# One attention and mixing kernel on one core: 24 float32 tiles of 32, smaller groups for scaling v, two weight tiles moved, all first shifts planned, filler products on TensorE

## The chip, the cores and the metric

One core of one Trainium2 chip. The metric is the device time of one execution, in microseconds (us); a profiled execution also gives a trace with every instruction of TensorE (PE), VectorE (DVE, Vector), ScalarE (ACT, Act), GpSimdE (POOL, Pool) and of the DMA queue of SyncE (SP).

## The reference

Three layers in a row. An attention over 2 batches of 8 heads, 768 rows of 64: query and key bits are the signs of six projections, and a score counts only where all six bits agree; then a softmax and the weighted sum of v. A channel layer with a time shift: `xk` and `xr` are mixtures of x and the row before it, `k = relu(xk @ w_k)`, `v = k*k @ w_v`, and the result is `sigmoid(xr @ w_r) * v`. A mixing layer: `u = x + (x^T U V)^T`, and the output is `u + relu(u @ w_ch1) @ w_ch2`. The weights reach the kernel as float64.

```python
mask = q_bucket[:, :, :, None] == k_bucket[:, :, None, :]
scores = np.where(mask, scale * np.matmul(q, k.transpose(0, 1, 3, 2)), -1000000000.0)
attn = np.exp(scores - np.max(scores, axis=-1, keepdims=True))
attn = attn / (np.sum(attn, axis=-1, keepdims=True) + 1e-09)
x = np.matmul(attn, v)                                   # then by batch, row, head*64
v = np.maximum(xk @ w_k, 0.0) ** 2 @ w_v
x = v / (1.0 + np.exp(-(xr @ w_r)))
u = x + (x.transpose(0, 2, 1) @ U @ V).transpose(0, 2, 1)
out = u + np.maximum(u @ w_ch1, 0.0) @ w_ch2
```

## The kernel before, in words

**Attention.** 16 heads of 6 query tiles, 96 tiles n = 6i + t. For each head q and k are loaded, split into a high and a low part (`prep_H`, `prep_L`), transposed on TensorE (`prep_T`), copied (`prep_E`), and the bits are made from a product (`prep_z`, `prep_bits`) and put beside the operands by DMA. For each tile: scores in four products of 384 columns (`scores`, lines 511 and 512), the row maximum on Vector (`row_max`, line 516) with two small steps, and the exponential on Act (`exps`, line 530). From there a tile goes one of two ways. A D tile is split into two fp16 parts (`part1` on Pool or Act, `part2` on Pool), transposed by a DMA (`transp`) and weighted with v in 18 fp16 products (line 577). A W tile (t = 1 and 4, `PE_TILES`) is transposed by TensorE in float32 (`flip`, line 556), copied out of PSUM by Act or Vector (`flip_out`) and weighted in 6 float32 products, 12 instructions (line 571). The sums of a head lie in one PSUM bank, `o`; at the head's end Vector reads it twice (`total`, line 584, and `normal`, line 596, with the reciprocal, line 588, between).

**v.** A power of two scales v for four heads together (`VG = 4`): Vector takes the largest value of each head's v (`v_max`, line 464), TensorE transposes the four maxima (`v_flip`, line 470), Vector makes the factor (`v_power`), TensorE spreads it (`v_spread`), Vector copies it (`v_scale`, line 487), and Act scales each head's v (line 496) before any tile of these heads can be weighted.

**Weights.** Each float64 weight tile is turned into two float32r parts in a chain: load, `conv_scale` on Act, `conv_bits` on Vector, `conv_sum` on Pool, and a split on Act and Vector or Pool. The first `JOBS = 8` tiles are made inside the attention; the others in ticks of the later loops, one stage of each per tick.

**The order.** The instructions of the attention are put in order by a planner (`Plan.order`, lines 75 to 125). It lists operations with costs for each engine, what they follow, which buffers (`SLOTS`) they take and free, and a due time (`DUE`, added to a step number); at each moment it starts what is ready and due first. Each engine runs its instructions in that order, so a wait holds everything behind it on that engine.

**The first shifts.** The channel layer of batch 0 needs 16 shifted inputs (`Mix.todo`: r and k, two halves of the rows, four chunks), each of which is scaled, summed, copied by Act (`shift_high`) and completed by Pool or Vector (`shift_low`). Twelve are in the plan, with the products for r (`r_step`); the last four, the second half for k, come after it, between the first half unit `k_half(mix, 0)` and the others. A unit m has two halves u = 2m and 2m + 1; the order of the halves, `u1`, is 0, 2, 1, 3, 4, ... The second products of a half (line 797 to 799, 9 of 512 columns) follow the first ones (12 of 384 columns) of the next half. The mixing layer at the end has 16 steps m for each group g of four row tiles, with the remaining weight tiles in ticks of g = 0.

## Time and profile before

| | us |
|---|---|
| median of 3 runs (739.63 to 741.1) | 739.86 |
| the profiled execution | 737.28 |
| its span, first to last instruction | 735.1 |
| busy in the span: PE, DVE, ACT, POOL | 701.2, 441.8, 384.8, 350.7 |
| mean granted clock of TensorE | 0.984 |

The attention ends at about 284 us, where the first unit of the channel layer starts. TensorE is busy for 95% of the span; busy times of products overlap, since they are pipelined, so the distance between starts tells more of their cost than their lengths. The trace names a line of the kernel and the tiles that an instruction writes and reads: `ps` and `pt` are PSUM tiles, `pT` a transposed tile, `xh` a split shifted input, `hl` a split first product, `nv` v in float32.

### The profile page before, as it was taken

What the parts mean: (1) busy time and instruction counts of PE and PEld (TensorE: products, weight loads), DVE (VectorE), ACT (ScalarE), POOL (GpSimd) and SP (SyncE); (2) the same over time, 40 slices, a digit from 0 to 9 for tenths busy, and PEclk for the clock granted to TensorE, in tenths of its full rate; (3) what the DMA queues carried; (4) which work ended last, traced back from release to release, by engine and by line L of the source; (5) the groups of instructions that cost most, each with busy time, mean ns of one, the idle gap of its engine ahead of it and who ended that gap; (6) DMA issues with size and microseconds to landing.
All of it is one profiled execution on the core that took longest, in us unless ns stands there. A gap on an engine that the chain in (4) does not pass through costs nothing.

```text
span 735.1 us, 12021 instructions
## 1 busy us (share of the span) xinstructions
PE 701.2 (95%) x4556; PEld 604.6 (82%) x4556; DVE 441.8 (60%) x791; ACT 384.8 (52%) x651; POOL 350.7 (48%) x308
## 2 busy tenths in 40 slices
PE   6879999998999998899999999999999999999997
PEld 6779988998899987788788888777888888888886
DVE  5868888777866575899779987845622111221112
ACT  3767878877878684676468656534421101210110
POOL 3879989876987774566347544623300000000000
PEclk9879999999999999899999999999999999999999
DMA  6688998898798792322012332322201000010001
GB/s 175 159 170 157 202 201 175 189 182 173 158 174 144 167 193 39 115 97 70 28 49 95 121 109 86 108 85 83 98 1 57 1 1 0 1 57 1 1 0 58
DMA packets 140714, 73.20 MB, mean 100 GB/s; under 512 B 116833, under 2 KB 134065, under 8 KB 140657
## 3 DMA queue, kind: packets, MB, share of 16 engines
q1 hardware_dynamic: 140512, 72.24, 42.1%
q8 instruction: 36, 0.59, 0.3%
q14 instruction: 22, 0.17, 0.1%
q10 hardware_dynamic: 144, 0.20, 0.1%
HBM read 37.10 MB, written 3.15 MB: 55 GB/s over the span
## 4 chain that ended last, share of the span: by engine, by line
PE 68%; POOL 10%; issue 6%; DVE 6%; DMA 5%; ACT 4%; SPq 0%; POOLq 0%; ACTq 0%; DVEq 0%
PE ps L797 9%; PE ps L799 9%; PE pt L797 9%; PE pt L799 9%; PE ps L798 9%; PE pt L798 9%; POOL p L179 4%; DMA pT<-p 3%; PE pt L571 3%; POOL p L381 2%; PE pt L577 2%; PE ps L511 2%; PE ps L512 2%; PE pt L405 1%; DVE w L179 1%
## 5 line engine op out<-in xcount | busy, mean ns | idle before, releaser
L872 DVE SCALAR_TENSOR_TENSOR hl<-pt,hl 128x512 fp32r<-128x512 f32 x48 | 33.2, 691 | 170.9 <-ACT hl L871 170.9
L871 ACT ACTIVATE hl<-pt 128x512 fp32r<-128x512 f32 x48 | 28.7, 598 | 186.1 <-PE pt L799 186.1
L799 PE MATMUL ps<-w,hl 128*128 128x512 f32 x288 | 114.3, 397 | 3.5 <-DVE hl L786 3.3
L797 PE MATMUL ps<-w,hl 128*128 128x512 f32 x288 | 115.6, 401 | 0.1
L798 PE MATMUL ps<-w,hl 128*128 128x512 f32 x288 | 113.7, 395 | 0.0
L179 POOL TENSOR_TENSOR cx<-cx,raw 128x512 int32<-128x512 int32 (+2 forms) x55 | 80.3, 1460 | 65.2 <-DVE cx L232 60.8
L179 POOL TENSOR_TENSOR p<-p,p 128x768 f16<-128x768 f32 x64 | 108.0, 1691 | 6.3 <-ACT p L379 4.5
L516 DVE TENSOR_REDUCE nm<-ps 128x1 f32<-128x768 f32 x96 | 90.5, 952 | 21.2 <-PE ps L512 19.2
L530 ACT ACTIVATE p<-ps,nm 128x768 f32<-128x768 f32 x96 | 92.8, 989 | 12.5 <-DVE nm L524 12.0
L511 PE MATMUL ps<-xk,xq 76*128 76x384 f32 x192 | 72.8, 379 | 3.4 <-ACT p L530 2.4
L797 PE MATMUL pt<-ut,w 128*128 128x512 f32 x192 | 75.6, 394 | 0.0
L799 PE MATMUL pt<-ut,w 128*128 128x512 f32 x192 | 75.0, 390 | 0.0
L798 PE MATMUL pt<-ut,w 128*128 128x512 f32 x192 | 75.0, 390 | 0.0
L799 PEld LDWEIGHTS ps<-w,hl 128*128 128x128 f32 x288 | 54.4, 189 | 19.4 <-DVE hl L786 7.4
L512 PE MATMUL ps<-yk,yq 128*128 128x384 f32 x192 | 67.2, 350 | 0.0
L797 PEld LDWEIGHTS ps<-w,hl 128*128 128x128 f32 x288 | 54.5, 189 | 14.2 <-issue 1.7
L179 DVE TENSOR_TENSOR w<-cx,w 128x512 fp32r<-128x512 f32 (+2 forms) x52 | 60.6, 1165 | 7.5 <-ACT w L272 7.1
L798 PEld LDWEIGHTS ps<-w,hl 128*128 128x128 f32 x288 | 54.6, 189 | 10.3
L577 PE MATMUL pt<-v,pT 128*128 128x65 f16 (+1 forms) x1152 | 47.3, 196 | 7.2 <-DMA pT<-p 5.2
L228 DVE SCALAR_TENSOR_TENSOR raw<-raw 128x512 uint32<-128x512 uint32 (+2 forms) x55 | 53.5, 973 | 0.0
L577 PEld LDWEIGHTS <-pT 128*128 128x128 f16 x1152 | 40.9, 99 | 13.9 <-issue 6.9
L381 POOL CAST p<-p 128x768 f16<-128x768 f32 x49 | 41.4, 846 | 22.1 <-ACT p L530 22.1
(178 smaller groups left out, 1478.1 us busy)
## 6 DMA issues: line engine op xcount, KB each, us to landing
raw<-in_moe_w_ch_dram SPq DMA_DIRECT2D x32, 512.0 KB
raw<-in_moe_w_k_dram SPq DMA_DIRECT2D x8, 512.0 KB
raw<-in_moe_w_v_dram SPq DMA_DIRECT2D x8, 512.0 KB
nk<-in_k_dram SPq DMA_DIRECT2D x16, 192.0 KB
nv<-in_v_dram SPq DMA_DIRECT2D x16, 192.0 KB
nq<-in_q_dram SPq DMA_DIRECT2D x15, 192.0 KB
xk<-yk SPq DMA_DIRECT2D x15, 192.0 KB
xq<-yq SPq DMA_DIRECT2D x15, 192.0 KB
```

The costliest lines, as they stand in the source:

```text
L179: eng.tensor_tensor(out=out, in0=a, in1=b, op=op)
L228: nc.vector.scalar_tensor_tensor(out=raw[:, :, 0], in0=raw[:, :, 1], scalar=0x80000000, in1=raw[:, :, 0], op0=ALU.bitwise_and, op1=ALU.bit ...
L381: (nc.vector if e == "dve" else nc.gpsimd).tensor_copy(dst, src)
L511: nc.tensor.matmul(s_ps[:, j, 0:G], d["xq"][:, qc], d["xk"][:, c], start=True, stop=False)
L512: nc.tensor.matmul(s_ps[:, j, 0:G], d["yq"][:, qc], d["yk"][:, c], start=False, stop=True)
L516: nc.vector.tensor_reduce(out=nm[:, 0:1], in_=tl[n]["s"][:, :, 0:G], axis=AX.XY, op=ALU.max, negate=True)
L530: nc.scalar.activation(p, tl[n].pop("s")[:, :, 0:G], AF.Exp, bias=nm[:, 2:3], scale=nm[:, 1:2])
L577: nc.tensor.matmul(o[:, 0:d], pT[:, part, kt, :], V[:, kt, a, 0:d], start=(kt == 0 and (part, a) == (0, 0)), stop=(kt == NT - 1 and part = ...
L797: nc.tensor.matmul(o, sh, mh, start=first, stop=False)
L798: nc.tensor.matmul(o, sh, ml, start=False, stop=False)
L799: nc.tensor.matmul(o, sl, mh, start=False, stop=last)
L872: nc.vector.scalar_tensor_tensor(out=hl[:, 1], in0=self.o, scalar=0.0, in1=f(hl)[:, 0], op0=ALU.max, op1=ALU.subtract)
```

## The change

- Tiles: `MODES` gives the way of each tile by batch and t. Batch 0 is D D W D D W, batch 1 is D D F D D W. An F tile is transposed by TensorE like a W tile; then Act takes its fp16 part out of PSUM (`flip_part1`), Vector subtracts it for the second part (`flip_part2`), and it is weighted by the 18 fp16 products of a D tile. So 24 of the 32 tiles that TensorE transposes stay float32.
- v is scaled in groups of 2, 2, 4, 4 and 4 heads (`GROUPS`).
- `JOBS` is 6: two weight tiles fewer in the attention. Two ticks (m = 4 and 6) are added in the mixing layer.
- All 16 first shifts are in the plan; the last four (`far`) wait for all scores and flips, because their buffers (`xh2`) take the place of the q and k preparation, whose tiles now have a pool of their own (`prep`) that is closed after the last score. The loop behind the plan is gone, and `u1` begins 0, 1, 2, ...
- Filler: before each operation of TensorE in the plan's order, a number of fp16 products of 128 x 128 ones with 120 columns is issued, 0.85 of the gap that the plan has there at 0.056 us each, and 34 ahead of the first. They write 120 spare columns of the bank of `o`, which is now one tile, `o_bank`, for all heads.
- The planner's costs of some operations and all due times are others.

```diff
@@ -20,18 +20,20 @@
 
-PE_TILES = (1, 4)
-DUE = {"ld": -28.3, "h": 7, "lo": 111.2, "tr": -11.5, "es": -25.5, "xs": 92.5, "z": -68.8, "bits": 0,
-       "mask": -276.3, "vm": -9.4, "v1": 6.8, "v2": -54.9, "sc": 55.7, "mx": 0.4, "sl": -2.6, "bi": -135,
-       "ex": 6.1, "fl": 48.2, "f1": 4.7, "p1": 52.8, "p2": 82.4, "T": -8, "av": 363.1, "nr": -62, "xp": 3.2,
-       "xe": -76.7, "j0": 20.9, "j1": 71.8, "j2": 329.8, "j3": 106.3, "j4": 470.2, "j5": 730.2, "j6": 845.8,
-       "j7": 172.1, "m0": -307, "m1": -117.4, "m2": 176.7, "r0": 344, "r1": 397.9, "r2": -42.6, "r3": -432.1,
-       "r4": -59.5, "r5": -145.5}
+MODES = ("DDWDDW", "DDFDDW")
+DUE = {"ld": -99.6, "h": -34.1, "lo": 130.6, "tr": 66.1, "es": -60.4, "xs": 46.6, "z": -218.4,
+       "bits": -138.8, "mask": -88.8, "vm": 17.4, "v1": 182.1, "v2": 335.9, "sc": 119.5, "mx": 10.9,
+       "sl": -3.2, "bi": -133.2, "ex": -22.6, "fl": 123.8, "f1": -95.5, "p1": 277.5, "p2": -1.3, "T": -77.7,
+       "av": 404.8, "nr": -45.7, "xp": 84.8, "xe": -119.1, "j0": 364.9, "j1": 212.6, "j2": 685.7,
+       "j3": 1005.2, "j4": 600, "j5": 738.7, "j6": 1882.5, "j7": -9.5, "m0": 30.4, "m1": -333.7, "m2": 373.4,
+       "r0": 351.9, "r1": 378, "r2": -841.9, "r3": -1555.3, "r4": -36.2, "fw": -86, "f2": -186.2,
+       "m3": 404.1, "r5": 0.4}
 JOB_GATE = (0, 0, 1, 1, 2, 3, 4, 5)
-JOBS = 8
-VG = 4
+JOBS = 6
+GROUPS = (2, 2, 4, 4, 4)
+FILL, FIRST_FILL = 0.85, 34
 SLOTS = {"s": 3, "t": 1, "o": 1, "n": 4, "hl_q": 1, "hl_k": 1, "y_q": 2, "y_k": 2, "x_q": 2, "x_k": 2, "zt": 2,
-         "p": 3, "p12": 4, "pT": 6, "xn": 2, "raw": 3, "cx": 4, "xh": 4, "sq": 3, "v": 2, "nm": 4, "nv": 6}
+         "p": 3, "p12": 4, "pT": 6, "xn": 2, "raw": 3, "cx": 4, "xh": 4, "xh2": 4, "sq": 3, "v": 2, "nm": 4, "nv": 6}
 
...
@@ -314,6 +318,8 @@
         nc.sync.dma_start(out=p_raw[r0:r0 + D, :], in_=proj)
+    steady = const.tile([128, 128], F16)
+    nc.gpsimd.memset(steady, 1.0)
     warm = const.tile([128, 1], F32)
...
@@ -321,6 +327,13 @@
     nc.gpsimd.tensor_copy(ident_r, ident)
+    o_bank = psum_t(512, "o")
+    spare = o_bank[:, NT * E1:NT * E1 + 120]
+
+    def idle_products(n):
+        for _ in range(n):
+            nc.tensor.matmul(spare, steady, steady[:, 0:120], start=True, stop=True)
+
     sgn = {"q": (-1.0, 1.0), "k": (1.0, -1.0)}
...
@@ -455,10 +468,12 @@
 
-    vg = [{} for _ in range(NH // VG)]
+    vg = [{} for _ in GROUPS]
+    vg_of = [(g, j) for g, n in enumerate(GROUPS) for j in range(n)]
+    VG = max(GROUPS)
 
     def v_max(i):
-        g, j = divmod(i, VG)
+        g, j = vg_of[i]
         if j == 0:
...
@@ -467,27 +482,28 @@
         vg[g]["t"] = psum_t()
-        nc.tensor.transpose(vg[g]["t"][0:VG, 0:128], vg[g].pop("max"), ident)
+        nc.tensor.transpose(vg[g]["t"][0:GROUPS[g], 0:128], vg[g].pop("max")[:, 0:GROUPS[g]], ident)
 
     def v_power(g):
-        m = ap.tile([VG, 1 + VG], F32, tag="vpow", name="vpow")
-        vg[g]["pow"] = m[:, 1:1 + VG]
+        n = GROUPS[g]
+        m = ap.tile([VG, 1 + VG], F32, tag="vpow", name="vpow")[0:n]
+        vg[g]["pow"] = m[:, 1:1 + n]
         m1 = m[:, 0:1]
-        nc.vector.tensor_reduce(out=m1, in_=vg[g].pop("t")[0:VG, 0:128], axis=AX.X, op=ALU.max)
+        nc.vector.tensor_reduce(out=m1, in_=vg[g].pop("t")[0:n, 0:128], axis=AX.X, op=ALU.max)
         nc.vector.tensor_scalar(m1, m1, 2.0 ** -100, None, ALU.max)
         nc.vector.tensor_scalar(words(m1), words(m1), 0x7F800000, 0x7F800000, ALU.bitwise_and, ALU.bitwise_xor)
-        nc.vector.tensor_scalar(vg[g]["pow"], ident[0:VG, 0:VG], m1, None, ALU.mult)
+        nc.vector.tensor_scalar(vg[g]["pow"], ident[0:n, 0:n], m1, None, ALU.mult)
 
     def v_spread(g):
         vg[g]["u"] = psum_t()
-        nc.tensor.matmul(vg[g]["u"][:, 0:VG], big, vg[g].pop("pow"), start=True, stop=True)
+        nc.tensor.matmul(vg[g]["u"][:, 0:GROUPS[g]], big[0:GROUPS[g]], vg[g].pop("pow"), start=True, stop=True)
 
     def v_scale(g):
-        sc = vg[g]["scale"] = ap.tile([128, VG], F32, tag="vsc", name="vsc", bufs=3)
-        nc.vector.tensor_copy(sc, vg[g].pop("u")[:, 0:VG])
+        sc = vg[g]["scale"] = ap.tile([128, VG], F32, tag="vsc", name="vsc", bufs=4)
+        nc.vector.tensor_copy(sc[:, 0:GROUPS[g]], vg[g].pop("u")[:, 0:GROUPS[g]])
 
     def v_scale_of(i):
-        g, j = divmod(i, VG)
+        g, j = vg_of[i]
         return vg[g]["scale"][:, j:j + 1]
...
@@ -510,6 +528,10 @@
             nc.tensor.matmul(s_ps[:, j, 0:G], d["yq"][:, qc], d["yk"][:, c], start=False, stop=True)
+        scored.append(n)
+        if len(scored) == NH * NT:
+            prep_s.close()
+            late["xh2"] = pool(mix_s, "xh2", bufs=4)
 
...
@@ -555,17 +577,33 @@
 
+    def mode(n):
+        return MODES[n // (NT * H)][n % NT]
+
     def flip_out(n, e):
         pT = tl[n]["pF"] = ap.tile([128, NT, 128], F32, tag="pT", name="pF", bufs=SLOTS["pT"])
         copy(e, pT.rearrange("p (j i) c -> p j (i c)", j=NG), tl[n].pop("f")[:, :, 0:G])
 
+    def flipped(n, part):
+        return tl[n]["pT"][:, part].rearrange("p (j i) c -> p j (i c)", j=NG), tl[n]["f"][:, :, 0:G]
+
+    def flip_part1(n):
+        pT_tile(n)
+        p1, src = flipped(n, 0)
+        nc.scalar.activation(p1, src, AF.Copy)
+
+    def flip_part2(n):
+        p1, src = flipped(n, 0)
+        minus("dve", flipped(n, 1)[0], src, p1)
+        tl[n].pop("f")
+
 
     def weighted(n):
         i, t = divmod(n, NT)
         if "o" not in hd[i]:
-            hd[i]["o"] = psum_t(NT * E1, "o").rearrange("p (t d) -> p t d", t=NT)
+            hd[i]["o"] = o_bank[:, 0:NT * E1].rearrange("p (t d) -> p t d", t=NT)
         o = hd[i]["o"][:, t]
-        if t in PE_TILES:
+        if mode(n) == "W":
             pT, v = tl[n].pop("pF"), NV[i % len(NV)]
...
@@ -945,18 +983,19 @@
         v_slots[i] = v_s, nv_s = Slot("v"), Slot("nv")
-        g, j = divmod(i, VG)
+        g, j = vg_of[i]
         ld = v_ld[i] = add({"sp": 0.74}, lambda e, i=i: load_head(i, "v"), ready_of[i - 4][1] if i >= 4 else [ld],
                            i * NT - 26 + 3 * j, take=[nv_s], issue=0.45)
         v_mx.append(add({"dve": 0.56}, lambda e, i=i: v_max(i), [ld], i * NT + 2 * j, "vm"))
-        if j == VG - 1:
-            at0 = g * VG * NT - 4
+        if j == GROUPS[g] - 1:
+            i0 = i - j
+            at0 = i0 * NT - 4
             t_s, u_s = Slot("t"), Slot("t")
-            fl = add({"pe": 0.2}, lambda e, g=g: v_flip(g), v_mx[-VG:], at0, take=[t_s], lag=0.25)
-            pw = add({"dve": 1.3}, lambda e, g=g: v_power(g), [fl], at0, free=[t_s])
+            fl = add({"pe": 0.2}, lambda e, g=g: v_flip(g), v_mx[i0:], at0, take=[t_s], lag=0.25)
+            pw = add({"dve": 1.5}, lambda e, g=g: v_power(g), [fl], at0, free=[t_s])
             sp = add({"pe": 0.2}, lambda e, g=g: v_spread(g), [pw], at0, take=[u_s], lag=0.25)
             v_sc = add({"dve": 0.15}, lambda e, g=g: v_scale(g), [sp], at0, free=[u_s])
-            for ii in range(g * VG, i + 1):
+            for ii in range(i0, i + 1):
                 v_s2, nv_s2 = v_slots[ii]
...
@@ -975,18 +1014,22 @@
             ex = add({"act": 1.02}, lambda e, n=n: exps(n), [bi], n, "ex", [p_s], [s_s, nm_s])
-            if t in PE_TILES:
+            kind = mode(n)
+            if kind in "FW":
                 f_s = Slot("s")
                 fl = add({"pe": 0.68}, lambda e, n=n: flip(n), [ex], n, "fl", [f_s], [p_s], lag=0.25)
                 last_s.append(fl)
-                got = add({"act": 0.83, "dve": 0.86}, lambda e, n=n: flip_out(n, e), [fl], n, "f1", [pT_s], [f_s])
+            if kind == "F":
+                p1 = add({"act": 0.83}, lambda e, n=n: flip_part1(n), [fl], n, "f1", [pT_s])
+                got = add({"dve": 0.97}, lambda e, n=n: flip_part2(n), [p1], n, "f2", free=[f_s])
+            elif kind == "W":
+                got = p1 = add({"act": 0.83, "dve": 0.95}, lambda e, n=n: flip_out(n, e), [fl], n, "fw", [pT_s], [f_s])
             else:
                 c_s = Slot("p12")
                 p1 = add({"act": 0.86, "pool": 0.85}, lambda e, n=n: part1(n, e), [ex], n, "p1", [c_s])
                 p2 = add({"pool": 1.7}, lambda e, n=n: part2(n), [p1], n, "p2", free=[p_s])
                 got = add({"sp": 2.2}, lambda e, n=n: transp(n), [p2], n, "T", [pT_s], [c_s], issue=1.45)
-            on_pe = t in PE_TILES
-            avs.append(add({"pe": 0.9 if on_pe else 0.62}, lambda e, n=n: weighted(n), [got, v0_of[i] if on_pe else v2], n, "av",
+            avs.append(add({"pe": 1.42 if kind == "W" else 0.62}, lambda e, n=n: weighted(n), [got, v0_of[i] if kind == "W" else v2], n, "av",
                            [] if avs else [o_s], [pT_s, v_s, v_slots[i][1]], lag=0.25))
...
@@ -1009,12 +1052,12 @@
         if j < JOBS + 2:
-            last = add({"dve": 1.75}, lambda e, j=j: conv_bits(j), [last], at, kind)
+            last = add({"dve": 2.2}, lambda e, j=j: conv_bits(j), [last], at, kind)
         if j < JOBS + 1:
             last = add({"pool": 1.32}, lambda e, j=j: conv_sum(j), [last], at, kind, free=[raw_s])
         if j < JOBS:
             h = add({"act": 0.65}, lambda e, j=j: conv_h(j), [last], at, kind)
-            done[j] = add({"dve": 1.1, "pool": 1.3}, lambda e, j=j: conv_l(j, e), [h], at, kind, free=[cx_s])
+            done[j] = add({"dve": 1.4, "pool": 1.3}, lambda e, j=j: conv_l(j, e), [h], at, kind, free=[cx_s])
     tick_n[0] = JOBS + 3
...
@@ -1024,14 +1067,16 @@
     hi = x_s = last = None
-    for j, (s, g, c) in enumerate(todo := mx0.todo[0:3 * KD]):
+    for j, (s, g, c) in enumerate(todo := mx0.todo):
         a_s = Slot("sq")
         if c == 0:
-            x_s = [Slot("xh") for _ in range(KD)]
+            far = (s, g) == ("k", 1)
+            x_s = [Slot("xh2" if far else "xh") for _ in range(KD)]
         at, kind, p = 2 * c, f"m{j // KD}", (s, g, c)
         begun = [add({"act": 0.6 if g else 0.85}, lambda e, p=p: mx0.shift_scaled(*p, e == "act"), begun, at, kind, [a_s])]
         sm = add({"dve": 1.1}, lambda e, p=p: mx0.shift_sum(*p), begun, at, kind)
-        hi = add({"act": 0.53}, lambda e, p=p: hold.append(mx0.shift_high(*p)), [sm, hi and low_of[todo[j - 1]]], at, kind, [x_s[c]])
+        hi = add({"act": 0.53}, lambda e, p=p: hold.append(mx0.shift_high(*p)), [sm, hi and low_of[todo[j - 1]], *(last_s if far else [])],
+                 at, kind, [x_s[c]])
         low_of[p] = add({"pool": 1.05}, lambda e, p=p: mx0.shift_low(*p, hold.pop(), nc.gpsimd), [hi], at, kind, free=[a_s])
...
@@ -1044,9 +1089,14 @@
                 add({"act": 0.62, "dve": 0.62}, lambda e, t=t: mx0.r_raw(t, e), [last], -40, f"r{t}", free=[t_s])
+    pe_end = None
     for op, e in plan.order():
+        if e == "pe":
+            gap = 0.0 if pe_end is None else op.end - op.on[e] - pe_end - 0.15
+            idle_products(FIRST_FILL if pe_end is None else int(max(0.0, gap) * FILL / 0.056))
+            pe_end = op.end
         op.fn(e)
-    mx0.todo = mx0.todo[3 * KD:]
+    mx0.todo = []
     att.close()
...
@@ -1082,7 +1131,7 @@
 
-    u1 = [0, 2, 1, 3, *range(4, U1 - 3), U1 - 2, U1 - 3, U1 - 1]
+    u1 = [*range(U1 - 3), U1 - 2, U1 - 3, U1 - 1]
 
...
@@ -1094,8 +1143,6 @@
     k_half(mix, 0, True)
-    while mix.todo or mix.begun:
-        shifts(mix, nc.gpsimd if len(mix.todo) % 2 else None)
     halves(mix, u1, range(1, U1 - 2), [(4, mix.r_out, 0, 2), (5, mix.r_out, 2, 2), (6, mix.r_out, 4, 2)] + [
...
@@ -1159,7 +1206,7 @@
                 tick()
-                if m in (8, 10, 12):
+                if m in (4, 6, 8, 10, 12):
                     tick()
```

## Rows read from the trace of the kernel before

**Rows 1.** Page, part 2: granted TensorE clock in 40 slices of 18.4 us, tenths

```profile
PEclk9879999999999999899999999999999999999999
```

**Rows 2.** Stretches: length; busy of PE, PEld, DVE, ACT, POOL (instructions); clock, DMA, GB/s

```profile
4.70:19.31 14.61, 13.07 (x47) 12.06 (x48) 9.76 (x20) 6.12 (x12) 4.34 (x7) 1.00 0.67 177
19.31:26.91 7.60, 5.73 (x32) 4.48 (x30) 6.03 (x16) 6.17 (x10) 5.05 (x6) 0.96 0.27 68
26.91:33.07 6.16, 6.16 (x24) 6.07 (x25) 6.16 (x7) 4.47 (x8) 6.08 (x5) 0.50 0.91 244
33.07:41.67 8.60, 4.84 (x27) 3.80 (x26) 8.29 (x21) 7.07 (x11) 7.96 (x7) 0.99 0.98 196
41.67:54.95 13.28, 11.35 (x98) 11.19 (x98) 7.91 (x12) 8.27 (x14) 9.37 (x7) 0.61 0.91 173
60.00:284.00 224.00, 213.53 (x2301) 199.13 (x2300) 166.05 (x380) 172.71 (x275) 185.62 (x155) 1.00 0.87 171
290.76:304.20 13.44, 10.52 (x35) 7.44 (x34) 12.80 (x15) 7.20 (x14) 9.03 (x7) 0.75 0.24 81
```

**Rows 3.** Timeline of TensorE, scores of two tiles: start, length, line, output and inputs

```profile
14.51 0.52 PE L512 MATMUL ps<-yk,yq 128*128 128x384 f32 x1
14.83 0.52 PE L511 MATMUL ps<-xk,xq 76*128 76x384 f32 x1
...
36.67 0.34 PE L511 MATMUL ps<-xk,xq 76*128 76x384 f32 x1
36.85 0.33 PE L512 MATMUL ps<-yk,yq 128*128 128x384 f32 x1
```

**Rows 4.** Timeline, v of the first heads: maximum, transpose of maxima, scale, first weighted product

```profile
9.40 0.54 DVE L464 TENSOR_REDUCE vmax<-nv 128x1 f32<-128x384 f32 x1
...
37.02 0.27 PE L470 MATMUL pt<-ident,vmax 128*4 128x128 f32 x1
...
41.38 0.14 DVE L487 COPY vsc<-pt 128x4 f32<-128x4 f32 x1
...
43.14 0.19 PE L577 MATMUL pt<-v,pT 128*128 128x65 f16 x1 [0.95 <-ACT v L498]
```

**Rows 5.** Busy time of line 516 alone (row maxima): length, DVE busy (instructions), clock, DMA

```profile
0.00:60.00 60.00, 13.61 (x15) 0.86 0.73 169
60.00:284.00 224.00, 76.94 (x82) 1.00 0.87 171
```

**Rows 6.** Timeline of TensorE: a float32 tile, an fp16 tile, then a flip

```profile
61.04 1.53 PE L571 MATMUL pt<-nv,pF 128*128 128x65 f32 x12
62.41 0.71 PE L577 MATMUL pt<-v,pT 128*128 128x65 f16 x18
62.95 0.85 PE L556 MATMUL ps<-ident,p 128*128 128x128 f32 x6
```

**Rows 7.** Groups by line: shapes, count, busy us, mean ns, idle before and releaser

```profile
L381 DVE COPY pF<-ps 128x768 f32<-128x768 f32 x12 | 11.4, 951 | 6.2 <-PE pt L571 5.1 <-PE ps L556 1.1
...
L596 DVE TENSOR_TENSOR xn<-pt,rl 128x384 f32<-128x384 f32 x16 | 8.9, 556 | 0.3
...
L584 DVE TENSOR_SCALAR rl<-pt,vsc 128x6 f32<-128x6 f32 x16 | 3.5, 219 | 10.2 <-PE pt L577 10.1
...
L588 DVE RECIPROCAL rl<-rl 128x6 f32<-128x6 f32 x16 | 3.0, 190 | 0.3
```

**Rows 8.** Timeline of TensorE, last flip and first steps of the mixing layer

```profile
271.83 0.82 PE L556 MATMUL ps<-ident,p 128*128 128x128 f32 x6
...
298.31 0.79 PE L799 MATMUL ps<-w,hl 128*128 128x512 f32 x1 [0.98 <-DVE hl L786]
...
304.20 0.39 PE L797 MATMUL ps<-w,hl 128*128 128x512 f32 x1
304.43 0.39 PE L798 MATMUL ps<-w,hl 128*128 128x512 f32 x1
```

**Rows 9.** Waits of TensorE from 60 to 284 us: total, times, longest us

```profile
PE pt L577 <- DMA pT<-p: 5.2, 6, 2.1
```

20 lines of the change are left out of this document (11 added, 9 removed).

## The prediction

> **What bounds the kernel now.** I read first the page's slices, then the busy time by stretch, then TensorE's timeline inside the stretches that stood out, then its waits. The slices show one clock dip at the start and one near 300 us [rows 1]. By stretch the run falls into three parts. From 60 to 284 us, the attention, TensorE is busy 213.5 of 224.0 us at full clock, with Pool at 185.6, Act at 172.7 and Vector at 166.1: TensorE is the bound, 10.5 us of it are idle, and the others are full enough that small delays reach it [rows 2]. The longest of its waits there is for the DMA transposes of fp16 tiles, 5.2 us in six waits [rows 9]. After 304 us TensorE hardly stops.
>
> The loss sits at two places. **The start**, 4.7 to 60 us: idle gaps of 1.5, 1.9, 0, 3.8 and 1.9 us, together 9.1 [rows 2], and long spells at the lower clock. Scores of 384 columns start 0.32 us apart at 14.5 us and 0.18 us apart at 36.7 us [rows 3]: 1.2 GHz against 2.4. The clock column says 1.00 before 19 us, but the distances say the lower level, and I go by them. The half-clock cost is at most half of the 13.07 us busy in the first stretch (6.5), 3.1 in the stretch granted 0.50, and 13.28 x 0.39 = 5.2 in the one granted 0.61: 14.8 us. Behind it stands a chain: the second head's maximum of v is begun at 9.40, yet the maxima are transposed at 37.02, the scale is copied at 41.38 and the first weighted product starts at 43.14 [rows 4], since a scale serves four heads and waits for the fourth v. **The start of the mixing layer**, 290.76 to 304.20: 13.44 us for the work of 24 products of 384 columns and 9 of 512. At 0.18 and 0.23 us each [rows 3, 8] that is 6.4 us. The rest, 7.0 us, is waiting for shifted inputs that are still being split, and a clock of 0.75 that follows the waits [rows 2, 8].
>
> **The change part by part.** The profiled execution took 737.28 us (span 735.1, 2.18 outside it); the median of three runs is 739.86, so 2.58 above it. I sum against 737.28 and add 2.58.
>
> *v in groups of 2, 2, 4, 4, 4, and products that fill the start.* The scale of heads 0 and 1 needs only maxima that exist at about 10 us, so the 43.14 ceases to be a gate and DMA transposes of the first fp16 tiles take its place. Price: 15 row maxima are issued by 60 us [rows 5], the other 81 by about the last flip at 271.83 [rows 8], which is 2.6 us a tile. Fifteen tiles at that pace are 39 us, so the start costs 21 us. It can't vanish: first scores stood at 14.1 us, after a chain of 9.4 us from 4.7 in which, by my estimate, Act and Vector hold two thirds. The clock takes half of the remaining third, 1.6 us, so some 12.5 us stay. I take 21 - 12.5 = 8 us gained; bounds 3 (the clock stays low, or Pool, busy 9.37 of 13.28 us while everything waits for v, becomes the limit at once) and 12. The 34 first products cost 34 x 0.10 us at the lower clock (120 columns, scaled from 0.32 us for 384 [rows 3]) = 3.4 us, hidden in the 4.7 us before TensorE's first work [rows 2]; if they start late, what sticks out delays the first transposes, 0 to 1 us. The fifth group adds four tiny Vector instructions and two tiny products, at 20 us, nothing on the path.
>
> *Eight F tiles for eight W tiles* (t = 2 of batch 1). The flip stays. A W tile takes 62.41 - 61.04 = 1.37 us of TensorE, a D or F tile 62.95 - 62.41 = 0.54 [rows 6]: 8 x 0.83 = 6.6 us. Vector pays 8 subtractions from PSUM, like the copy of 951 ns [rows 7], 7.6 us in all less the copies it made before, and row maxima queue behind them. I take 6 gained, bounds 1 and 6.6: the stretch is TensorE's. The other 24 W tiles only move from t = 1, 4 to t = 2, 5.
>
> *All first shifts planned, and the order of the first units put straight.* It removes the 7.0 us above. The last four shifts now follow the last score and flip, each an Act copy and then a Pool subtraction in a chain of about 1.7 us, 6.8 us together; from the last flip at 271.83 to 284 there were 12 us of other TensorE work, and unit 1 needs them 2 us later still. So I cost them at nothing; if Pool is late, up to 3 us come back. I take 6.5; bounds 3.5 and 7.0.
>
> *Two weight tiles fewer in the attention.* Two loads, scalings, bit steps, sums and splits leave Act, Vector and Pool there, and go to the channel layer as two more ticks (m = 4, 6), where Vector and Act are nearly idle. The split of a weight now comes two half units ahead of its use, not four; a half unit is about 4 us and the split under 2. I take 0, bounds -1 (a late split) and +2.
>
> *Idle products in the plan's gaps.* They cost nothing where TensorE really waits and 0.056 us each where it doesn't. TensorE's idle time from 4.7 us to 284 is about 20 us (9.1 + 10.5); 85% of as much would be 17 us of products, some 300. Since the plan's gaps and the real ones are alike only in part, but the plan's costs for W tiles and bit steps now lie nearer to the measured ones, I take 2.5 lost; bounds 0 and 17.
>
> *Where the products land.* They write columns of the very bank that holds the weighted sums, which Vector reads at each head's end for 0.22 + 0.19 + 0.56 = 0.97 us (total, reciprocal, product) [rows 7]. Products issued after these reads in program order, but meant for a gap inside them, hold TensorE until Vector is done, and every later product behind them. No row of before shows it, since nothing but the next head's sums waited there. Bounds 0 and 16 x 0.97 = 15.5 us; I take 3, as most reads end in gaps that the plan saw too. The Trainium skill says under PSUM — Partial Sum Buffer, Terms, that an engine reading a bank while TensorE writes the same bank and partitions is a collision, so the accesses must be kept apart in time. By that rule each of the 16 heads can pay the whole read, and the sum would be 12.5 us worse; no run shows it yet.
>
> *New due times.* They reorder everything; the 10.5 us of waits could halve or grow by half, 0 taken, bounds -5 and +5.
>
> Sum: 8 + 6 + 6.5 - 2.5 - 3 = 15 us. 737.28 - 15 = 722.3; with 2.58: **about 725**.
>
> On the clock, the trace has TensorE busy 11.35 of 13.28 us from 41.67 to 54.95, with 65-column products and transposes, at 0.61 [rows 2]. The Trainium skill, TensorE: Matmul & The Clock Gate, Part 1, says that the throttled state is the default and sustained activity releases it. By that alone this stretch should have been at full speed soon; the row shows a stretch that stayed low while the engine was busy, so I can't count on the products to lift it, and rival (a) stands for that.
>
> **The rivals.** (a) *The clock doesn't rise at the start*: the fill doesn't do what it says. For it: the stretch at 0.61 although busy. Against: 384-column scores were followed by a rise near 19 us. The start then gains 3: 730. (b) *Products run on a busy engine*: if the real gaps lie elsewhere than the planned ones, 17 us are paid in place of 2.5: 739. Against it: the first 12 us and the start's gaps are real. (c) *Slower: TensorE held at the bank.* Place: the end of each head. If Vector has one row maximum (about 0.95 us, 76.94 / 82 [rows 5]) ahead of the reads, a head costs 1.92 us, 16 heads 31 us; without this term the gain is 18, so it is slower from 1.13 us a head on. At 1.92: 739.9 - 18 + 31 = 753. Against it: heads end while Vector has slack (166 of 224), and only a gap planned just there makes a product wait. (d) *More*: start 12, waits for other engines reduced by 5, products free: 4 + 5 + 2.5 = 11.5 more, 713.
>
> **How the numbers follow.** Forecast (717 to 731) 0.58; (a) 0.10, inside that span; (b) 0.10, from 734 to 743; (c) 0.09; (d) 0.13, from 705 to 717. What a measurement can tell from no change is about 0.2%, 1.5 us: 738.4 to 741.3. Faster: 0.58 + 0.10 + 0.13 + half of (b) = 0.86; same: 0.04 of (b); slower: (c) and 0.01 of (b), 0.10. The range leaves out (c), the upper half of (b) and the end of (d): 708 to 738.
>
> **What would show it.** Right: first weighted product before 30 us; scores 0.18 us apart by the first tile; first mixing unit near 272 us, no gaps in its first 20 us; no row in which TensorE waits for lines 584 or 596. Wrong: waits for these lines; products with other work already ready behind them; a clock below 0.9 in the first 60 us; the last shifts ending after the mixing layer has begun.

## The result and the profile after

The changed kernel takes 743.41 us (median of 16 runs, 741.08 to 751.52), the kernel before 738.89 beside it. The ratio is 1.0082, 95% interval 1.0055 to 1.0109: slower by 6.1 us, where 15 us less were forecast (the medians lie 4.5 us apart; the ratio leaves out executions in a slower state). The profiled execution took 743.95 us, with a span of 742.0.

The start did what the prediction wanted. TensorE's timeline (start, length, line, operation, tiles, count, and in brackets the wait and what ended it) begins with the 34 products, and the row maxima of the first 60 us follow (count; shortest, median and longest ns; first and last start):

```profile
0.98 3.58 PE L335 MATMUL pt<-steady 128*128 128x120 f16 x34 [0.98 <-POOL warm L324]
...
7.66 0.34 PE L456 MATMUL ps<-yq,wb_rest_q 128*108 128x384 f32 x1
7.84 0.34 PE L456 MATMUL ps<-yk,wb_both_k 128*108 128x384 f32 x1
...
23.39 0.72 PE L615 MATMUL pt<-v,pT 128*128 128x65 f16 x18
```

```profile
L538 DVE TENSOR_REDUCE nm<-ps x18: 935/948/958, 13.1 to 54.6; 128x1 f32<-128x768 f32 x18
```

Products of 384 columns start 0.18 us apart from the beginning, the first weighted product is at 23.39 us and no longer at 43.14 [rows 4], and 18 row maxima are begun by 60 us in place of 15 [rows 5]: three tiles at 2.6 us, 7.8 us, just what the first term said. But the last of the 18 starts at 54.65 and the next one at 64.91. Ten us without a row maximum follow, and most of the lead is gone: the nineteenth is 2.5 us ahead of the one before (67.38), the eighteenth was 11.4 ahead (66.07 before). The timelines of SyncE's queue and of the engines that feed it or wait for it show what stood there:

```profile
47.95 6.61 SPq L567 DMA_TRANSPOSE pT<-p  x2
54.65 0.55 SPq L447 DMA_DIRECT2D xk<-yk  x1
55.30 0.54 SPq L447 DMA_DIRECT2D xq<-yq  x1
55.94 1.77 SPq L567 DMA_TRANSPOSE pT<-p  x1
57.81 1.70 SPq L467 DMA_DIRECT2D xk<-zt  x2
59.56 1.49 SPq L467 DMA_DIRECT2D xq<-zt  x2
61.09 0.52 SPq L311 DMA_DIRECT2D nk<-in_k_dram  x1
...
49.34 1.65 POOL L181 TENSOR_TENSOR p<-p,p 128x768 f16<-128x768 f32 x1
...
53.00 0.68 DVE L460 TENSOR_SCALAR zt<-pt,thr 108x384 fp32r<-108x384 f32 x1 [1.15 <-PE pt L456]
...
64.30 0.53 ACT L392 ACTIVATE hl_k<-nk 128x384 fp32r<-128x384 f32 x1 [4.50 <-DMA nk<-in_k_dram]
```

The four mask transfers of the next head (467) have their data from 53.7 us, when Vector has written `zt`, but they are issued only from 57.81 to 61.05, and the load of a later k (311) comes behind them. Ahead of them stand three DMA transposes (567) and two copies. These transposes don't wait for Pool: taken in order, none of the 64 transposes of after begins before Pool's second part of its tile is done, and the ninth, at 55.94, has its part from 50.99. The queue itself is late; the transfers begun from 41.67 to 54.95 take 1.10 times what the 16 DMA engines have there. Act waits 4.50 us for that k, Vector 3.43 us for the next scores, and TensorE 2.08 us before them (the view names nothing for this wait), until about 64 us.

The rest of the lead goes later. The 51st row maximum is still 3.9 us ahead (145.24 against 149.15); the 52nd starts 9.67 us behind it and is 3.4 late. Between them TensorE waits for a transpose that lands 5.09 us after its issue (first row, from the chain of waits), and Vector for a v and for the next scores:

```profile
143.22 5.09 DMA pT<-p
...
148.36 1.17 PE L615 MATMUL pt<-v,pT 128*128 128x65 f16 x18 [2.12 <-DMA pT<-p]
...
150.63 0.55 DVE L479 TENSOR_REDUCE vmax<-nv 128x1 f32<-128x384 f32 x1 [4.01 <-DMA nv<-in_v_dram]
154.91 0.96 DVE L538 TENSOR_REDUCE nm<-ps 128x1 f32<-128x768 f32 x1 [3.73 <-PE ps L530]
```

By the 70th the new kernel is 11.3 us late, at the last of the 96 it is 6.4.

The stretches by busy time (columns as in rows 2):

```profile
60.00:284.00 224.00, 206.17 (x2205) 192.41 (x2203) 154.78 (x355) 165.26 (x260) 172.84 (x144) 0.95 0.85 161
150.00:155.00 5.00, 5.00 (x28) 4.69 (x28) 0.64 (x2) 3.32 (x6) 1.56 (x2) 0.50 0.51 110
301.31:314.75 13.44, 13.44 (x69) 12.17 (x68) 13.07 (x15) 9.10 (x17) 8.90 (x8) 1.00 0.43 132
```

From 60 to 284 us every engine does less than before [rows 2], TensorE 206.2 for 213.5 and Pool 172.8 for 185.6, and the clock falls to 0.95. The worst place is at 150 us, at half clock and with Vector nearly idle. The first unit of the channel layer starts at 294.46 us, not at 283.91. The third row is the start of the mixing, laid as far behind that first unit as the stretch of before was: TensorE is busy all of the 13.44 us at full clock, where before it was 10.52 at 0.75 [rows 2].

The waits from 60 us to there (waiting engine, tile and line, what ended it: us in total, times, longest):

```profile
PE pt L615 <- DMA pT<-p: 6.3, 6, 2.1
PE pt L335 <- DVE rl L622: 3.7, 5, 1.2
...
PE pt L335 <- DVE xn L634: 1.6, 3, 1.1
...
PE pt L335 <- DVE nm L542: 0.7, 1, 0.7
```

```profile
DVE vmax L479 <- DMA nv<-in_v_dram: 14.2, 7, 4.0
```

Line 335 is the filler: its products wait 6.0 us in nine places for Vector, eight of them for the reads of the shared bank. Vector waits 14.2 us for v to be loaded, 5.7 before:

```profile
DVE vmax L464 <- DMA nv<-in_v_dram: 5.7, 5, 1.8
```

### The profile page after: what moved, and what is told of

Its sections match the earlier page's. It is cut to its first block, busy times and chain, and to the rows that moved or that the text cites. A ratio compares the mean times of both kernels' runs of the same rounds, so it can differ in the third digit from the quotient of the medians.

```text
span 742.0 us, 12789 instructions
## 1 busy us (share of the span) xinstructions
PE 707.8 (95%) x4936; PEld 612.3 (83%) x4936; DVE 444.4 (60%) x793; ACT 391.2 (53%) x660; POOL 354.3 (48%) x311
## 4 chain that ended last, share of the span: by engine, by line
PE 67%; DVE 9%; POOL 9%; issue 5%; ACT 4%; DMA 4%; SPq 1%; POOLq 0%; DVEq 0%; ACTq 0%
PE ps L835 9%; PE ps L837 9%; PE ps L836 8%; PE pt L835 8%; PE pt L837 8%; PE pt L836 8%; POOL p L181 3%; PE pt L615 3%; PE ps L529 3%; PE ps L530 2%; POOL p L394 2%; PE pt L609 2%; PE pt L456 2%; DMA pT<-p 2%; DVE w L181 1%
## 5 line engine op out<-in xcount | busy, mean ns | idle before, releaser
L529 PE MATMUL ps<-xk,xq 76*128 76x384 f32 x192 | 71.2, 371 | 4.9 <-ACT p L552 2.5
L181 DVE TENSOR_TENSOR w<-cx,w 128x512 fp32r<-128x512 f32 (+2 forms) x52 | 59.1, 1136 | 6.9 <-ACT w L276 6.8
L232 DVE SCALAR_TENSOR_TENSOR raw<-raw 128x512 uint32<-128x512 uint32 (+2 forms) x55 | 60.5, 1099 | 0.0
L615 PE MATMUL pt<-v,pT 128*128 128x65 f16 x1296 | 52.5, 196 | 7.0 <-DMA pT<-p 6.5
L615 PEld LDWEIGHTS <-pT 128*128 128x128 f16 x1296 | 45.7, 99 | 14.9 <-DMA pT<-p 9.1
```

Of the source, the lines that this page charges most:

```text
L181: eng.tensor_tensor(out=out, in0=a, in1=b, op=op)
L232: nc.vector.scalar_tensor_tensor(out=raw[:, :, 0], in0=raw[:, :, 1], scalar=0x80000000, in1=raw[:, :, 0], op0=ALU.bitwise_and, op1=ALU.bit ...
L529: nc.tensor.matmul(s_ps[:, j, 0:G], d["xq"][:, qc], d["xk"][:, c], start=True, stop=False)
L615: nc.tensor.matmul(o[:, 0:d], pT[:, part, kt, :], V[:, kt, a, 0:d], start=(kt == 0 and (part, a) == (0, 0)), stop=(kt == NT - 1 and part = ...
```

## The experiments

All ratios are to runs of the kernel before on the same chip, with the 95% interval. "The kernel n6" and so on are the names of the runs.

| run | what | ratio | interval |
|---|---|---|---|
| after | the change | 1.0082 | 1.0055 to 1.0109 |
| n1 | no products at all | 1.0022 | 0.9984 to 1.0060 |
| n2 | products only to 60 us | 0.9991 | 0.9955 to 1.0028 |
| n3 | v loads earlier | 1.0023 | 0.9981 to 1.0065 |
| n4 | F tiles done as W tiles | 1.0061 | 1.0023 to 1.0100 |
| n5 | n2 and n3 together | 1.0004 | 0.9976 to 1.0031 |
| n6 | no products behind the heads' reads | 0.9977 | 0.9943 to 1.0011 |
| n7 | n1 and n3 together | 0.9997 | 0.9967 to 1.0026 |
| n13 | n6 and n3 together | 0.9989 | 0.9957 to 1.0021 |
| n14 | n6, other due times | 1.0027 | 0.9995 to 1.0059 |
| n16 | of the later products only those behind the reads | 1.0085 | 1.0056 to 1.0114 |
| n15 | n6, 48 DMA transposes halved | 0.9836 | 0.9786 to 0.9886 |
| n17 | n6, 10.5 MB more to transfer | 1.0160 | 1.0116 to 1.0205 |
| n18 | n6, 60 issues more on SyncE's queue | 1.0552 | 1.0504 to 1.0600 |
| n8 | before, 34 products at its start | 1.0043 | 1.0005 to 1.0080 |
| n9 | before, half of the float32 products | 0.9922 | 0.9892 to 0.9951 |
| n10 | before, 48 DMA transposes halved | 0.9918 | 0.9881 to 0.9956 |
| n11 | before, half of each row maximum | 1.0011 | 0.9962 to 1.0060 |
| n12 | before, copies for Pool's subtractions | 1.0044 | 1.0006 to 1.0081 |

### The products: length or bank (n1, n2, n6, n16)

Theory A was that the products cost the time, theory B that the new order with its late loads does. n1 sets the filler to nothing, n2 keeps it for operations that the plan ends before 60 us:

```diff
-FILL, FIRST_FILL = 0.85, 34
+FILL, FIRST_FILL = 0.0, 0
```

> The changed kernel without any filler product, everything else in the same order. Its trace holds 329 products, 195 of them in the first 60 us; behind 60 us they cost about 8 us of TensorE, and six waits of 5 to 6 us in all for the head's end on VectorE. Theory A (the products cost what the start gained): 733 to 738, the loss at the start (clock low again, about 3 us) less than what comes back. Theory B (the order is at fault: loads and preparations that land later than the plan has them hold the in-order engines): 743 to 748, since the stalls stay and the start loses its clock.

> The changed kernel with products only where the plan's time is below 60 us; the start keeps its clock. Theory A: 730 to 735, 8 to 13 us less than the changed kernel. Theory B: 739 to 743, a gain of no more than 4 us, because the stalls near 62, 148 and 200 us and the half clock that follows them stay.

Both come back to the time before. n1 (739.39 us) falls between the times of the two theories and n2 (738.78) just under those of B, so neither theory holds as it stood. All products together cost 0.6%, 4.4 us. n2, which keeps those of the first 60 us, isn't slower than n1, so what they cost lies behind 60 us. n6 then leaves out the products that would stand ahead of the first TensorE work behind a head's total, reciprocal and product (kind `nr`), 108 of 329; n16 leaves out all others but the first 34:

```diff
+        read = read or op.kind == "nr"
         if e == "pe":
-            idle_products(FIRST_FILL if pe_end is None else int(max(0.0, gap) * FILL / 0.056))
+            idle_products(FIRST_FILL if pe_end is None else 0 if read else int(max(0.0, gap) * FILL / 0.056))
+            read = False
```

> The changed kernel without the products that would stand ahead of the first TensorE work behind each head's total, reciprocal and product (the reads of the shared bank); all others stay. Theory 1 (the loss by products is the wait at the bank, 6 us of such waits in the trace): 737 to 740 us, with no rows in which a product waits for Vector. Rival (the loss is the length of the products that run while other work is ready): 742 to 744, and the bank's waits are replaced by waits for other engines.

> The complement of n6: of the products, only the 34 first ones and those ahead of the first TensorE work behind each head's total, reciprocal and product (some 108). Theory 1 (the bank's wait is the cost): as slow as the changed kernel, a ratio of 1.006 to 1.010. Rival (the length of all products, the bank's wait being filled by other waits): 1.001 to 1.004, since only a third of the products after the first is left.

The two complements part cleanly. With the products behind the reads alone the kernel is as slow as with all of them (1.0085, 1.0082), without them it is 0.9977: 1.05% less, 7.7 us, with an error of some 0.4% either way. n16's waits are those of after, n6 has none of them:

```profile
PE pt L335 <- DVE rl L622: 2.5, 4, 1.1
PE pt L335 <- DVE xn L634: 1.6, 3, 1.1
...
PE pt L335 <- DVE nm L542: 0.7, 1, 0.7
```

So length is not the cost; the place is. That it is the shared bank follows from the rows (the products wait there for Vector's readers of that bank); a filler in another bank at the same place wasn't tried, since the attention's other PSUM tiles hold all the other banks. The Trainium skill, under PSUM — Partial Sum Buffer, Terms, calls it a collision, and an error, when TensorE writes a bank while Vector reads the same bank and partitions. The eight waits for the reads, 5.3 us, are what keeping the two apart costs TensorE here.

### The v loads and the due times (n3, n5, n7, n13, n14)

In after, v's loads stand in SyncE's queue behind runs of DMA transposes, whose due times fell from n - 8 to n - 77.7 while v's hardly moved. n3 moves each v load, from the third head on, to the first place that its buffer and its heads allow:

```diff
+        if i > 1:
+            ordered.insert(first, ordered.pop(now))
```

> The changed kernel with each load of v (from the third head on) moved ahead in SyncE's queue as far as its buffer and its predecessors allow, past up to four other entries, most of them DMA transposes; all other engines keep their order. In the changed kernel VectorE stands 14.2 us in seven waits for v, against 5.7 us before. Theory A: no difference, 741 to 745. Theory B: these waits fall below 5 us, and 4 to 10 us of the time with them, 734 to 739.

> Products only where the plan ends before 60 us, and the v loads from the third head on taken ahead in SyncE's queue; nothing else differs from the changed kernel. Theory 1 (the two losses lie in different places and add): 1.0082 - 0.009 - 0.006, a ratio near 0.993 (some 734 us), with the channel layer's first k unit at 280 to 284 us. Rival (both only let the same waiting move to the next place, since Vector, Act and Pool set the pace from 20 us on): a ratio near 0.999 (738), with the first k unit at 286 to 289, and the rows of waiting for v gone but those for the row maxima and for the exponentials longer by as much.

> No products at all, and the v loads from the third head on taken ahead in SyncE's queue. If the products' start is worth what n2 against n1 seemed to show (0.3% at most), this comes within 0.3% of the kernel with products to 60 us and v loads ahead; theory 1: 0.993 to 0.997; the rival of that run (the same waiting moves on): 0.999 to 1.003.

> The changed kernel without the products at the heads' reads, and the v loads from the third head on taken ahead in SyncE's queue. Theory 1 (the loads' order costs where a head's v comes late, and nothing else of n6 is moved): a ratio of 0.992 to 0.995 to the kernel before. Rival (as with the kernels of products to 60 us, n2 and n5, the loads' order is worth nothing): 0.997 to 1.000.

Vector's wait for v falls from 14.2 us to 5.7, and after itself gains 0.6%. But on top of n1, n2 or n6 the same move gives -0.25, +0.1 and +0.1%, nothing. The theory that the two losses add is refuted: with the products out of the way Vector waits 12.7 us for v in n6 and 5.8 in n13, at the same time of the kernel. A late v no longer sets it.

n14 gives n6 other due times, found by search on a model of the plan in which TensorE's last operation of the attention came 10.6 us earlier:

> n6's instructions in an order from other due times, found by search on a model of the plan with costs nearer to the measured ones (row-wise work of Vector and Pool 4% longer, SyncE's issues 8%). The model has TensorE's last operation of the attention 10.6 us earlier than with the change's due times. Theory 1 (the order by due times sets the attention's length, and the changed one is no better than the old): 0.985 to 0.993. Rival (a model's gain is not the chip's: order found by search on a list of costs brings as much as it loses): 0.998 to 1.015.

It came out 0.5% slower than n6. The plan's own end is no safe measure of the chip's: an order that is shorter in the list of costs need not be shorter on the chip.

### F tiles and what bounds the attention (n4, n9, n11, n12)

n4 keeps after's order and its products, but copies the eight F tiles out and weights them in float32 like W tiles:

```diff
-        if mode(n) == "W":
+        if mode(n) in "FW":
```

> The changed kernel with the eight F tiles handled as W tiles in the same places of the order: no fp16 part on ScalarE, a copy in place of the subtraction on VectorE, float32 products. TensorE does 8 x 0.83 = 6.6 us more, ScalarE 8 x 0.8 us less. If TensorE is the bound of batch 1: 748 to 751. If waits for other engines hold batch 1: 742 to 745.

TensorE has 42.7 us of float32 products there and 33.4 in after, and 37.4 us of fp16 products in place of 42.2: 4.5 us more by distances of starts. The time is not longer (1.0061). The F tiles gave no gain that shows. To see why, parts of the work of before were left out, in before's order: half of the float32 products (n9), half of the columns of each row maximum (n11), half of Pool's time for the second parts (n12).

```diff
-            for kt in range(NT):
+            for kt in range(3):
```

> The kernel before, in its own order, with only three of the six float32 products of each W tile (the other half of the weighted sum is left out): some 21.6 us of TensorE's own work less (half of the 43.2 us of weighted float32 products by distances of starts), nothing else changed. Theory 1 (the prediction's view, TensorE is the bound of the attention): a gain of 15 to 20 us, 717 to 723. Rival (TensorE only follows: its waits take up what its work gives back): a gain under 6 us, with TensorE's waits in the attention longer by 15 us.

> The kernel before with each row maximum over half of its columns (so the exponentials are not scaled by the true maximum): some 0.45 us less in each of 96, 40 us of Vector's work. Theory (Vector's row maxima stand in the chain from scores to exponentials and set the pace): a gain of 8 us or more. Rival: under 3 us.

> The kernel before with Pool's 64 subtractions of 1.69 us replaced by its copies of 0.85 us (the second fp16 part is then a copy of the tile and not its remainder): 54 us of Pool's work less. Theory (Pool sets the pace in the attention): a gain of 8 us or more. Rival: under 3 us.

Of 21.6 us of TensorE's work 5.8 come back (0.78%), a little over a quarter; of 40 us of Vector's and 54 us of Pool's nothing does. n9's waits have grown: TensorE's gaps from 60 us to the first unit are 17.6 us in n9 and 10.5 in before, and the wait for the transposes has doubled, 5.2 before [rows 9]. That is a part of the rest; the remainder wasn't followed.

```profile
PE pt L577 <- DMA pT<-p: 10.4, 6, 2.6
```

So TensorE is not the bound of the attention, though it is busy 213.5 of 224 us. The same can be read from before's chain of waits from 60 to 280 us, which the prediction didn't use (shares of the stretch by line; the end is cut off by the view):

```profile
by line: POOL p L179 12.6%; issue 11.3%; DMA pT<-p 9.3%; PE pt L571 8.9%; PE pt L577 7.5%; POOL p L381 6.7%; PE ps L511 5.3%; PE ps L512 4.8%; PE ps L556 3.5%; PE pt L443 3.3%; ACT p L530 3.1%; PE pt L405 2.9%; PE pt L797 2.6%; PE pt L798 2
```

Pool's parts (lines 179 and 381) and the transposes hold 28.6% of it, and the TensorE lines that are shown only some 40%. The share of Pool is not what it seems: the view names the last instruction of Pool that ended while a transpose was issued. In before, too, no transpose begins ahead of its own second part, and only 8 of the 57 behind 60 us begin right at its end; the others have their data and stand in SyncE's queue (2.9 us in the median of all 57). n12, without a gain from 54 us less of Pool's work, says the same.

### SyncE's queue and the DMA engines (n10, n15, n17, n18)

The page's busy rows don't count instructions that issue DMAs. Added up issue by issue, SyncE's queue is busy 179 of 220 us between 60 and 280 in before, 181 in after and 184 in n6, and the DMA engines are busy for 0.88, 0.84 and 0.87 of these stretches. n10 (on before) and n15 (on n6) transpose only the first of two parts from tile 24 on:

```diff
+        k = 1 if n >= 24 else 2
         nc.sync.dma_start_transpose(
-            out=pT_tile(n).rearrange("p a b c -> p (a b) c"),
+            out=pT_tile(n)[:, 0:k].rearrange("p a b c -> p (a b) c"),
```

> The kernel before with the DMA transposes of tiles 24 and up cut to the first of their two parts (48 of 64 transposes halved; the products of the second part read the first, so TensorE's work is the same, and the result lacks the second part). DMA engines are 0.73 to 0.96 busy in the attention of before. Theory (the DMA engines and SyncE's queue set the pace there): a gain of 8 us or more. Rival (they don't: an engine does): under 3 us.

> n6 with the DMA transposes of tiles 24 and up cut to their first part (48 of 64; the result lacks the second part, TensorE's work is the same). The kernel before gained 0.8% by this. Theory (the new order is held by the DMA transposes and SyncE's queue at least as much): 0.985 to 0.990 to the kernel before, 0.8 to 1.2% under n6. Rival (its stalls lie elsewhere): within 0.4% of n6, 0.994 to 0.999.

Both gain, before 0.8%, 6.1 us, and n6 1.4%, 10.4 us; n10 falls between its two theories. That the new order is held by its transposes more than the old one is not shown, since the two gains agree within their errors (0.4 and 0.6%). The issue of one falls from 1.82 to 1.25 us (medians of n6 and n15 in the last rows of this section), and the DMA engines' share from 0.87 to 0.61. n15 is the shortest kernel of this study, 724.25 us, but it computes with less of each exponential. The queue's issues between 60 and 280 us fall by 23 us in n10 and by 37 in n15, so that a us less of them goes with 0.26 to 0.28 us of gain, about as much as a us of TensorE in n9. The edit takes away three things at once: bytes, issue time and a wait, because a transpose of the first part alone need not wait for Pool's second part (14 and 16 of them begin before it is done). n12, where that part comes 0.85 us sooner without a gain, speaks against the wait.

n17 and n18 try bytes and issues one by one. n17 adds transfers from Act's queue, n18 splits each mask transfer of SyncE in two:

```diff
+            nc.scalar.dma_start(
+                out=out[i % 2].rearrange("(p x) d -> p (x d)", x=NT)[:, 0:4 * NT * D].rearrange("p (h e) -> p h e", h=4),
+                in_=q[i % 2, 0:4].rearrange("h (p t) d -> p h (t d)", t=NT),
+            )
```

```diff
+            for c in (0, G // 2):
                 nc.sync.dma_start(
-                    out=f(hd[i]["x" + s])[D:MC, g * G:(g + 1) * G], in_=f(hd[i]["zt"])[z:z + 2 * NB]
+                    out=f(hd[i]["x" + s])[D:MC, g * G + c:g * G + c + G // 2],
+                    in_=f(hd[i]["zt"])[z:z + 2 * NB, c:c + G // 2],
```

> n6 with 14 additional transfers of 0.75 MB (from q to a part of the output that the kernel overwrites at its end), one behind each head's v from the third on, issued from Act's queue (0.41 us each for its one load at the start of before: some 6 us of Act). 10.5 MB more for the DMA engines in the attention, about a quarter, and nothing more on SyncE's queue. Theory D (the DMA engines hold the order): slower than n6 by 0.8% or more, 1.006 to 1.015 to the kernel before. Theory S (SyncE's queue holds it): within 0.4% of n6, 0.995 to 1.002.

> n6 with each of the masks' transfers on SyncE's queue split into two of half the columns: 60 issues more at 0.5 to 0.8 us, 30 to 48 us of SyncE's queue, which is about 188 of 220 us busy with n6 in the attention, and no bytes more. Theory S (SyncE's queue): slower than n6 by 1% or more, 1.008 to 1.02 to the kernel before. Theory D (the DMA engines): within 0.4% of n6, 0.995 to 1.002.

Both additions make the kernel slower than n6, and each by more than its theory had forecast. In n18 the masks take 91.2 us of SyncE's queue, 47.6 in n6, and the kernel 5.75%, 42.4 us more: nearly 1 us for each us. The stretches from 60 to 280 us of n6, n15, n17 and n18, in this order:

```profile
60.00:280.00 220.00, 202.64 (x2249) 187.76 (x2247) 161.44 (x365) 170.22 (x274) 178.43 (x149) 0.98 0.87 165
```

```profile
60.00:280.00 220.00, 208.48 (x2297) 194.72 (x2296) 167.46 (x372) 176.70 (x285) 183.93 (x154) 0.98 0.61 124
```

```profile
60.00:280.00 220.00, 197.99 (x2081) 185.94 (x2079) 153.51 (x353) 162.26 (x255) 170.79 (x144) 0.95 0.95 195
```

```profile
60.00:280.00 220.00, 187.91 (x1859) 177.16 (x1856) 129.62 (x308) 144.58 (x227) 150.47 (x125) 0.88 0.70 135
```

and the transposes in SyncE's queue behind 60 us (line, count, shortest, median and longest ns, first and last start) of before, after, n6, n15 and n18:

```profile
L545 SPq DMA_TRANSPOSE pT<-p x57: 1302/1718/2747, 64.0 to 273.8; - x57
```

```profile
L567 SPq DMA_TRANSPOSE pT<-p x55: 1276/1732/4433, 63.1 to 282.1; - x55
```

```profile
L567 SPq DMA_TRANSPOSE pT<-p x55: 1310/1819/4781, 61.9 to 271.3; - x55
```

```profile
L568 SPq DMA_TRANSPOSE pT<-p x55: 1210/1247/2763, 62.0 to 263.0; - x55
```

```profile
L569 SPq DMA_TRANSPOSE pT<-p x55: 1414/1857/4797, 61.1 to 316.5; - x55
```

In n18 the DMA engines are less busy (0.70) and every engine does less. A transpose that has its data stands 5.5 us in the queue in the median, 2.6 in n6, and TensorE's waits for transposes and masks grow (first row n6, the others n18, both from 60 to 294 us):

```profile
PE pt L615 <- DMA pT<-p: 6.9, 8, 1.8
...
PE pt L617 <- DMA pT<-p: 16.5, 8, 4.3
PE ps L531 <- DMA xq<-zt: 4.5, 4, 2.3
```

So the attention follows SyncE's queue there. But these issues stand right ahead of a head's first scores, and the masks of a head take 6.1 to 6.9 us from first to last in n18, 3.1 to 3.7 in n6; issues added at another place of the queue weren't tried. In n17 the engines' share rises to 0.95, and 13.5 us are lost, of which Act's 14 issues of 0.58 us may be a part. From the first to the last transpose the interval is 3.75 us each in before (209.8 / 56), 4.06 in after, 3.88 in n6 and 3.72 in n15. The Trainium skill, Trainium Kernel Development and Optimization, Key Constraints, says that all queues share the DMA engines and that issuing from several only saves the sequencer's issue time. Here an addition to that time came back nearly in full (n18). A kernel with the masks issued from another queue wasn't tried.

### The clock at the start alone (n8)

The 34 products ahead of before's first work, its order as it was:

> The kernel before with only the 34 first products of 120 columns ahead of TensorE's first work, in its own order. Theory 1 (the start is set by the chain of loads, Act, Vector and Pool, not by TensorE's clock): scores at 0.18 us from the first, first weighted product still near 43, and a gain of 0 to 1 us (0.9987 to 1.000). Rival (the prediction's step: a clock at full level is worth 4 to 5 us at the start): 733 to 735 us.

Neither: 0.4% slower. The products lift the clock, and it falls back in the first small gaps, at 8.5 us:

```profile
7.80 0.40 PE L445 MATMUL ps<-yq,wb_both_q 128*108 128x384 f32 x1 [0.56 <-ACT yq L381]
8.03 0.35 PE L445 MATMUL ps<-yq,wb_rest_q 128*108 128x384 f32 x1
8.21 0.49 PE L445 MATMUL ps<-yk,wb_both_k 128*108 128x384 f32 x1
8.50 0.52 PE L445 MATMUL ps<-yk,wb_rest_k 128*108 128x384 f32 x1
8.82 0.52 PE L445 MATMUL ps<-yq,wb_both_q 128*108 128x384 f32 x1
```

Starts 0.18 us apart become 0.32 apart, 1.2 GHz. In after the same products run without that fall, with filler in these gaps, and in n1, with none, the thirteenth row maximum comes at 46.8 in place of 43.5. The filler at the start works and gives 3 us there; the waiting at 55 to 65 us takes them, and the nineteenth comes at 65.2 in n1 and at 64.9 in after.

## Why the prediction was wrong

**What bounds the kernel: wrong, and the root of the rest.** The prediction took TensorE's 213.5 busy of 224 us for the bound and priced all TensorE time at full value. n9 shows that a us taken from TensorE gives 0.27 us. A us taken from SyncE's queue gives about as much (n10, n15), but a us put on it costs nearly one (n18), and bytes cost too (n17). So the attention has no single bound, and what the prediction left out is the queue: the new due times reorder it, and their term was put at 0 from TensorE's waits alone. The Trainium skill, Trainium Kernel Development and Optimization, Best Practices, warns against judging the distance to the roofline by matmul busy time; it names MFU and weight loads instead. Weight loads, 199.1 of 224 us in the same row [rows 2], would have pointed at TensorE as well. What could have told it is the queue's timeline, the DMA share of 0.87 in that row, and small trials like n9.

**Start, +8: right at 60 us, lost later.** The three tiles of lead were there. The step that failed is the silent one, that tiles go on at 2.6 us each once begun. At 65 us 2.5 us of the lead were left, since masks and the next k came late through SyncE's queue, behind transposes that had long had their data. The rest went between 145 and 155 us, at a late transpose and a late v, and more after it.

**F tiles, +6 (1 to 6.6): nothing that shows.** At n9's rate 6.6 us of TensorE are worth 1.8; n4 against after shows no gain, within 0.5%. TensorE's own work up to the first unit of the channel layer did fall, from 260.3 to 248.8 us by distances of starts; waits, lead-in and products together grew from 23.6 to 45.7.

**Planned shifts, +6.5 (3.5 to 7.0): 3.6.** From the first unit to the end it is 447.6 us, 451.2 before. The other traces agree: 447.5 to 447.7 in all twelve with the change's due times, 450.7 to 451.1 in the five of the old order (450.3 in n14). The 7.0 us of gaps and low clock are gone, as the stretch at 301.31 shows. In the unit ahead of it TensorE is busy 5.71 of 6.85 us, 6.63 before; 1.14 of that is a wait for Vector at 300.50. Pool is busy 6.24 us there, 1.35 before, with the last two shifts among its work, and Vector's subtraction stands behind two bit steps of 1.80 and 1.04 us, which took 0.68 and 0.42 at the same place before (last row: before). That Pool makes them longer fits, but wasn't tested, and where the rest of the 2.9 us went stays open.

```profile
295.73 1.01 POOL L181 TENSOR_TENSOR xh<-xs_a,xh 128x384 fp32r<-128x384 f32 x1 [0.16 <-ACT xh L765]
...
297.21 1.80 DVE L232 SCALAR_TENSOR_TENSOR raw<-raw 128x512 uint32<-128x512 uint32 x1
...
285.85 0.68 DVE L228 SCALAR_TENSOR_TENSOR raw<-raw 128x512 uint32<-128x512 uint32 x1
```

**Idle products -2.5 and the bank -3: the sum nearly right, the parts not.** All products together cost 4.4 us (n1), 5.5 were forecast. The bank's part is 7.7 us (n6), 0.48 us a head and inside its bounds of 0 and 15.5, and the rest of the products gave back some 3 us, which the intervals of n1 and n6 don't quite secure. Rival (c) was the right mechanism at less than half of the 1.13 us a head from which it alone would have turned the sign; the other gains had to fail too.

**Due times, 0 (-5 to +5), and two weight tiles, 0.** With 3.6 gained, 4.4 lost and 0 to 1.8 for the F tiles, 5.3 to 7.1 us are lost in all the rest, the start included. Set against the start's +8 that is 13 to 15 us for the order, far beyond the bound of 5; it is where the start's lead went. The places at 65 and 150 us and n15, n17 and n18 point at transfers and SyncE's queue as what carries it; that is argued, not shown. Which due time is to blame stays open, and two weight tiles fewer weren't tried by themselves.

**The range and the signs.** 743 lies beyond 738, the upper end. The 0.86 for faster rested on three gains; one was priced in TensorE's time, and another counted on tiles that follow at its pace. Of the signs named beforehand, the waits at the reads, the products with other work ready (at 293.37 below) and the late first unit came true, and the last shift ended at 296.74, behind the first unit's start at 294.46; the clock below 0.9 in the first 60 us did not.

```profile
291.93 1.26 PE L335 MATMUL pt<-steady 128*128 128x120 f16 x21 [1.13 <-DVE xn L634]
293.03 0.50 PE L644 MATMUL pt<-ident,xn 128*128 128x128 f32 x3
293.37 1.00 PE L335 MATMUL pt<-steady 128*128 128x120 f16 x16
```

No kernel of the study that does the whole work is measurably faster than the one before: n6 is within its error (0.9977, up to 1.0011).
